# Reordering the first loads of a Strassen cross-network kernel, and holding back its first writes

## The chip, the cores and the metric

The kernel runs on one core of one Trainium2 chip. The metric is the device time of one execution, in microseconds; lower is better. Before the change it took 2280.2 us (median of 3 runs, 2279.63 to 2280.74).

## The reference, cut to what matters

```python
B, F, D, L = 16384, 100, 16, 6
Din = min(F * D, 1024)                       # 1024
# x0: (16384, 1024), ws: (6, 1024, 1024), bs: (6, 1024), all bf16
def reference(x0, ws, bs):
    x = x0
    for l in range(6):
        proj = jnp.einsum('bd,de->be', x, ws[l]) + bs[l]
        x = x0 * proj + x
    return x
```

## The kernel before

The batch is cut into 16 pairs of 512-row blocks. One *unit* is one layer of one pair: units 0 to 5 are the six layers of the first pair, units 6 to 11 those of the second, and so on, 96 in all. Each unit multiplies a 1024x1024 activation block by a 1024x1024 weight by Strassen's scheme. The weight's quadrants are called `1`, `w12`, `2` and `4`; seven products P1 to P7 use quadrants or sums of them. The sums (*combinations*) are `5 = w12 + 4`, `6 = 5 - 1`, `7 = 1 - w12`, `3 = 2 - 6`, and `2i` and `5i`, sums inside `2` and `5` for a second level of the scheme that later pairs use. The activation side has sums T1 to T4. In the first pair VectorE (DVE) makes the weight combinations, and the GpSimd queue writes them to the DRAM tensor `Lc`, from which later pairs load them.

All operations are put in one list with a rank each; an engine issues its operations in order of rank, so a rank table is the order of each engine.

```python
    # how the first pair makes and writes combinations
    RAW = [("1", "load"), ("2", "load"), ("4", "load"), ("w12", "stage")]     # order of a layer's raw loads
    def combo(name, w, a, b, o_, deps, ...):
        def fn():
            t = ring_make(u, w)
            tt(t[:], raw(a)[:], raw(b)[:], o_)                                 # DVE
            nc.gpsimd.dma_start(Lc[...], t[:])                                 # written at once
        add(name, fn, ...)
    # ... c5 of layer 0 is made in two halves (c5, c5b); 2i and 5i go to the buffers isum[2 * (l % 2)],
    # isum[2 * (l % 2) + 1], which every second layer uses again

    # ... the start of the program
    for w in ("1", "2"):
        nc.scalar.dma_start(wt[(0, w)][:], w_src(0, w))                        # 512 KB each, ScalarE queue
    nc.scalar.dma_start(b_rows[:], bs...)                                      # 12 KB
    load_half(nc.scalar, "w12", 0)                                             # 256 KB
    load_half(nc.scalar, "4", 0)
    load_quarter(0, 0)                                                         # x0 quarters, 512 KB each,
    load_quarter(1, 0)                                                         # DMA transposes, SyncE queue
    load_quarter(0, 1)
    load_half(nc.sync, "w12", 1)
    load_half(nc.sync, "4", 1)
    load_quarter(1, 1)
    nc.tensor.matmul(pX[3][:, 0:48], lhsT=b_rows[:], rhs=ident[0:48, 0:48], ...)
    nc.vector.tensor_copy(out=b_all[:], in_=pX[3][:, 0:48])
```

In layer 0, P1 needs quadrant `1` and x0 quarter (0,0); P2 needs `2` and quarter (1,0); P5 needs the first half of combination 5 and T1 (quarter (0,1)), then the second half; P6 needs combination 6 and T2 (quarter (1,1)). So all of x0's four quarters and all four raw quadrants, 4 MB, have to land before P6.

## Time and profile before

| | before |
|---|---|
| time, median of 3 | 2280.2 us |
| span in the profile | 2279.1 us |
| TensorE busy | 2252.4 us |
| first useful matmul | 9.20 us |
| first matmul of layer 0's P5 / P6 | 17.54 / 22.12 us |
| first matmul of layer 1's P5 | 44.48 us |

Two lines of the page, before (the busy time of each engine, and the shares of the chain of work that ended last):

```profile
PE 2252.4 (99%) x12713; PEld 1263.8 (55%) x12951; DVE 2079.8 (91%) x2326; ACT 1841.2 (81%) x3228; POOL 20.0 (1%) x42
...
PE 96%; DVE 1%; SPq 1%; issue 1%; DMA 1%; ACT 0%; DVEq 0%; ACTq 0%
```

The kernel is bound by TensorE (PE). What PE waits for in the whole execution, before (who waits, for whom, us in total, times, longest):

```profile
PE pX L558 <- DMA b_rows<-in_bs_dram: 3.3, 1, 3.3
PE pX L284 <- DVE T L197: 2.6, 2, 1.5
PE pX L531 <- DVE zeros L528: 1.2, 1, 1.2
PE pX L284 <- DVE wp L197: 0.9, 1, 0.9
PE pX L396 <- DVE ti L197: 0.2, 1, 0.2
```

L558 is the small matmul with the bias rows, L284 the matmuls of P1 to P7, L531 warm-up matmuls. Where these waits stand, in the timeline, before (start us, length us, engine, line, operation, count, and in brackets the idle time before it and what ended it; `wp` is a raw weight or a combination, `w` is w12):

```profile
9.07 0.19 PE L558 MATMUL pX<-ident,b_rows 48*128 48x48 bf16 x1 [3.28 <-DMA b_rows<-in_bs_dram]
9.20 3.63 PE L284 MATMUL pA<-x0T,wp 128*128 128x512 bf16 x16
...
17.54 1.04 PE L284 MATMUL pX<-T,wp 128*128 128x512 bf16 x3 [1.15 <-DVE T L197]
...
19.52 2.76 PE L284 MATMUL pX<-T,wp 128*128 128x512 bf16 x12 [0.94 <-DVE wp L197]
...
22.12 8.80 PE L284 MATMUL pA<-T,wp 128*128 128x512 bf16 x39
...
31.73 1.23 DVE L197 TENSOR_TENSOR wp<-w,wp 128x2048 bf16<-128x2048 bf16 x1 [2.36 <-DMA w<-in_ws_dram]
...
43.21 1.23 DVE L197 TENSOR_TENSOR T<-xst 128x2048 bf16<-128x2048 bf16 x1
...
44.48 3.61 PE L284 MATMUL pX<-T,wp 128*128 128x512 bf16 x16 [1.48 <-DVE T L197]
```

Read it so: 16 matmuls of 128x512 take 3.63 us, one each 216 ns. PE starts useful work at 9.20, stops twice around P5 of layer 0, once before P5 of layer 1, and, but for 0.2 us (the `ti` line above), never again until the tail. At 31.73 DVE makes layer 1's combination 5. This stands in DVE's order before layer 0's last outputs, so the outputs, then layer 1's T1 (43.21), then PE at 44.48 are late.

### The profile page before, as it was taken

Reading aid. Unit: us, or ns where it says so; the run is one execution under the profiler, and the core shown is the slowest. Engines: PE = TensorE matmul, PEld = TensorE weight load, DVE = VectorE, ACT = ScalarE, POOL = GpSimd, SP = SyncE. Lnnn points to the kernel's source line nnn. Section 1 sums busy time; section 2 is a strip of 40 time slices with the busy share of each in tenths; the row PEclk is TensorE's granted clock in tenths of the full one; section 3 lists DMA queues with packets and bytes.
Section 4 is the critical chain, followed back from the end, with each engine's and each line's share of the span. In section 5 each row is a group of like instructions: output and inputs, shape, how many; then the busy total and the mean of one; then the engine's idle time right before and its main releaser. Section 6 shows DMA issues by size and latency. Waiting matters only on the chain.

```text
span 2279.1 us, 34736 instructions
## 1 busy us (share of the span) xinstructions
PE 2252.4 (99%) x12713; PEld 1263.8 (55%) x12951; DVE 2079.8 (91%) x2326; ACT 1841.2 (81%) x3228; POOL 20.0 (1%) x42
## 2 busy tenths in 40 slices
PE   8999999999999999999999999999999999999998
PEld 3455555555555555555555555555555555555554
DVE  6999999999999999999999999999999999999997
ACT  5678888878888888888888888888888888888887
POOL 1110000000000000000000000000000000000000
PEclk9999999999999999999999999999999999999999
DMA  9869797796977969779697796978969689696872
GB/s 276 241 232 291 271 252 266 211 311 196 247 263 215 302 212 250 258 225 283 215 263 250 226 282 214 262 252 226 284 204 285 233 230 284 195 293 227 240 241 66
DMA packets 625868, 557.01 MB, mean 244 GB/s; under 512 B 397600, under 2 KB 552224, under 8 KB 625696
## 3 DMA queue, kind: packets, MB, share of 16 engines
q1 hardware_dynamic: 617808, 534.05, 79.1%
q0 software_dynamic: 5184, 18.88, 2.1%
q10 hardware_dynamic: 2704, 1.85, 0.3%
q8 instruction: 101, 1.65, 0.3%
q14 instruction: 71, 0.58, 0.1%
HBM read 436.22 MB, written 52.43 MB: 214 GB/s over the span
## 4 chain that ended last, share of the span: by engine, by line
PE 96%; DVE 1%; SPq 1%; issue 1%; DMA 1%; ACT 0%; DVEq 0%; ACTq 0%
PE pA L284 56%; PE pX L396 24%; PE pX L284 16%; DVE ev L197 1%; SPq L534 1%; DMA w<-in_ws_dram 1%; DVE xst L197 0%; ACT ev L293 0%; DVE T L197 0%; DVE isum L197 0%; SPq L547 0%; SPq L245 0%; DVE wp L197 0%; DVE x0T L494 0%; ACT pX L289 0%
## 5 line engine op out<-in xcount | busy, mean ns | idle before, releaser
L284 PEld LDWEIGHTS <-wp 128*128 128x128 bf16 x7904 | 772.3, 98 | 843.0 <-issue 2.9
L284 PE MATMUL pA<-T,wp 128*128 128x512 bf16 x4471 | 1048.6, 379 | 7.2
L293 ACT ACTIVATE ev<-pA,b_all 128x512 bf16<-128x512 f32 x1124 | 706.2, 691 | 212.1 <-PE pA L284 166.3
L396 PEld LDWEIGHTS <-wp 128*128 128x128 bf16 x4984 | 487.0, 98 | 158.3 <-issue 16.1
L197 DVE TENSOR_TENSOR ev<-ev,x0T 128x2048 bf16<-128x2048 bf16 (+2 forms) x484 | 483.2, 1000 | 7.9 <-ACT ev L293 1.3
L197 DVE TENSOR_TENSOR xst<-ev,xst 128x2048 bf16<-128x2048 bf16 x319 | 389.2, 1220 | 18.8 <-DVE ev L197 0.5
L396 PE MATMUL pX<-ti,wp 128*128 128x256 bf16 x2848 | 397.9, 272 | 0.2 <-DVE ti L197 0.2
L197 DVE TENSOR_TENSOR ev<-ev,ev 128x2048 bf16<-128x2048 bf16 (+1 forms) x283 | 343.9, 1215 | 25.5 <-ACT ev L293 7.4
L293 ACT ACTIVATE ev<-pX,b_all 128x512 bf16<-128x512 f32 x412 | 288.9, 706 | 61.4 <-PE pX L284 51.3
L284 PE MATMUL pX<-xst,wp 128*128 128x512 bf16 x1369 | 335.8, 379 | 0.3
L284 PE MATMUL pA<-xst,wp 128*128 128x512 bf16 x1205 | 302.3, 379 | 4.0
L289 ACT COPY pX<-pA 128x512 f32<-128x512 f32 x412 | 256.7, 627 | 39.9 <-PE pA L284 39.9
L289 ACT CAST ev<-pX 128x512 bf16<-128x512 f32 x384 | 225.1, 620 | 52.2 <-ACT ev L293 37.3
L197 DVE TENSOR_TENSOR ev<-iu,ip 128x1024 bf16<-128x1024 bf16 x178 | 122.6, 689 | 120.5 <-ACT iu L289 120.4
L289 ACT COPY pX<-pX 128x512 f32<-128x512 f32 x356 | 208.7, 587 | 8.3
L289 ACT CAST iu<-pX 128x512 bf16<-128x512 f32 x356 | 197.1, 639 | 1.0 <-PE pX L396 0.9
L197 DVE TENSOR_TENSOR T<-xst 128x2048 bf16<-128x2048 bf16 x160 | 194.9, 1218 | 0.3
L197 DVE TENSOR_TENSOR T<-xst,T 128x2048 bf16<-128x2048 bf16 x160 | 194.8, 1218 | 0.2
L396 PE MATMUL pX<-T,wp 128*128 128x256 bf16 x1068 | 160.2, 273 | 0.0
L289 ACT CAST ip<-pX 128x512 bf16<-128x512 f32 x178 | 104.8, 589 | 53.7 <-PE pX L396 53.7
L396 PE MATMUL pX<-xst,wp 128*128 128x256 bf16 x888 | 133.2, 273 | 0.0
L197 DVE TENSOR_TENSOR xst<-ev,x0T 128x2048 bf16<-128x2048 bf16 x64 | 78.3, 1223 | 1.5
(44 smaller groups left out, 621.2 us busy)
## 6 DMA issues: line engine op xcount, KB each, us to landing
wp<-Lc SPq DMA_DIRECT2D x538, 512.0 KB, 4.6
wp<-in_ws_dram SPq DMA_DIRECT2D x285, 512.0 KB, 5.4
out_dram<-x0T SPq DMA_DIRECT2D x30, 1024.0 KB, 8.4
Lc<-wp POOLq DMA_DIRECT2D x24, 512.0 KB, 6.2
Lc<-isum POOLq DMA_DIRECT2D x12, 512.0 KB, 5.5
w<-in_ws_dram SPq DMA_DIRECT2D x5, 512.0 KB, 9.3
wp<-in_ws_dram ACTq DMA_DIRECT2D x2, 512.0 KB, 5.3
out_dram<-x0T SPq DMA_DIRECT2D x2, 512.0 KB, 3.4
```

Source lines behind the costliest of these rows:

```text
L197: nc.vector.tensor_tensor(out=o, in0=a, in1=b, op=op)
L284: nc.tensor.matmul(bank[:], lhsT=wt[(u, w)][:, k, m * P:(m + 1) * P], rhs=rhs[:, k, :], start=(start and k == 0), stop=(k == KH - 1), skip ...
L289: add(name, lambda: nc.scalar.copy(out=dst, in_=src), rd, wr)
L293: add(name, lambda: nc.scalar.activation(out=dst, in_=src, func=IDENT, bias=b_all[:, c:c + 1], scale=1.0), rd, wr)
L396: nc.tensor.matmul(pX[bank][:, m * NQ:(m + 1) * NQ], lhsT=wv[:, k, m * P:(m + 1) * P], rhs=rhs[:, k, :], start=(start and m == 0 and k == ...
L534: nc.sync.dma_start_transpose(out=blk(x0Ts[0], dh, n), in_=x0[n * NB:(n + 1) * NB, dh * H:(dh + 1) * H])
```

## The change

The intent is to get the first products going sooner and to keep the early writes out of the way of the loads:

- Bias rows first on the ScalarE queue, then quadrants `1` and `2`. Both halves of w12 and `4` go to the SyncE queue, after three x0 quarters.
- The writes of the first pair's combinations become operations of their own, with ranks. The six of layer 0 also wait for a *gate*, a 128x1 copy on GpSimd that reads the first quarter of layer 0's result.
- Later layers' raw weights are loaded in the order `4`, `w12`, `1`, `2`.
- New rank tables for units 0 to 7, so a new order on PE, ScalarE and DVE. In layer 0, T1 now stands before combination 5, and `2i` is finished late.

```diff
-    RAW = [("1", "load"), ("2", "load"), ("4", "load"), ("w12", "stage")]
+    RAW = [("4", "load"), ("w12", "stage"), ("1", "load"), ("2", "load")]
@@ the rank table of unit 0, its DVE part (those of units 1 to 7 are replaced likewise; PE and ScalarE parts cut)
-2i5@-7.88 2i6@-7.41 2i3@-6.94 2i7@-6.47 c5@4.62 T1@5.76 c5b@7.12 c6@7.86 T2@9.00 T3@10.13 Qm@11.27 c7@12.40 c3@13.67
-T4@14.81 Qa@15.94 5i5@17.41 5i6@19.06 ...
+2i5@-9.73 T1@3.57 2i7@4.71 2i6@5.04 c5@5.67 c5b@7.37 c6@8.11 T2@9.25 c7@10.38 T3@11.52 T4@12.65 2i3@13.79 c3@14.12
+Qm@15.26 5i5@17.53 Va@19.74 Qa@20.88 ...
@@ writes
-                    nc.gpsimd.dma_start(Lc[units[u][1], CIDX[w]].rearrange("p (k e) -> p k e", k=KH), t[:])
+            def save(w, t, rd, weights=(), l=l):
+                def fn():
+                    nc.gpsimd.dma_start(Lc[l, CIDX[w]].rearrange("p (k e) -> p k e", k=KH), t()[:])
+                if first:
+                    late.append(lambda add=add: add("s" + w, fn, rd + ["gate"], (), weights))
+                else:
+                    add("s" + w, fn, rd, (), weights)
+            if first:
+                gate = const.tile([P, 1], BF16, name="gate")
+                late.append(lambda ...: add("gate", lambda: nc.gpsimd.tensor_copy(gate[:], xst[:, 0, 0, 0:1]), [XO[0, 0]], ["gate"]))
@@ the start of the program
+    nc.scalar.dma_start(b_rows[:], bs.rearrange("l (m p) -> (l m) p", p=P))
     for w in ("1", "2"):
         nc.scalar.dma_start(wt[(0, w)][:], w_src(0, w))
-    nc.scalar.dma_start(b_rows[:], bs.rearrange("l (m p) -> (l m) p", p=P))
-    load_half(nc.scalar, "w12", 0)
-    load_half(nc.scalar, "4", 0)
     load_quarter(0, 0)
     load_quarter(1, 0)
     load_quarter(0, 1)
-    load_half(nc.sync, "w12", 1)
-    load_half(nc.sync, "4", 1)
+    for h in range(2):
+        load_half("w12", h)
+        load_half("4", h)
     load_quarter(1, 1)
@@ the bias matmul writes a bank of pA in place of pX
```

## The prediction

> **What bounds the kernel now.** TensorE. The page gives PE 2252.4 us busy of a 2279.1 us span, and the chain that ended last is 96% PE. In the timeline the 512-column matmuls start every 216 ns without a break, apart from the start-up and three gaps. The view of waits, for PE, lists 8.2 us in all: 3.3 us for the bias rows' DMA (before the first useful matmul at 9.19 us), 2.6 us in two waits for a T tile from DVE (about 1.2 us at 17.54, P5 of layer 0; about 1.5 us at 44.48, P5 of layer 1), 0.9 us for the second half of combination 5 (at 19.52). Then nothing stops PE until the tail, which the change leaves alone.
>
> So only the first 45 us can be won. After the first matmul there are about 3.5 us of gaps; ahead of it little: the bias rows (issued at 1.75, landing 7.3 us later, 9.05) end the wait, but the first x0 quarter (0.74 + 8.2 = 8.9) lands only 0.15 us sooner.
>
> **What the change moves.**
> - No arithmetic goes; one 128x1 copy on POOL is added.
> - The bias rows go ahead of the weights on the ScalarE queue. Worth 0.1 to 0.6 us.
> - 512 KB (first halves of w12 and 4) leave the ScalarE queue and come after three x0 quarters on SyncE. In the DMA view, 8 to 10 us, the ScalarE queue moved 0.47 MB and the SyncE queue 0.05 MB, while the second quarter was outstanding. [...] Quarters landed at 8.9, 12.6, 16.1 and 20.7 us. A quarter alone took about 2 us (0.48 to 0.52 MB in the stretches 10 to 12 and 12 to 14). Estimate after: 8.6, 11, 13.3, about 19.5.
> - Price: both halves of combination 5 are later. Estimate: first half of w12 and 4 landed at 15.5, combined (0.69 us) by 16.2; second by 18. P1 and P2 (3.45 us each) end at 15.6; P5 starts near 16.3 instead of 17.54.
> - P6 needs T2, hence the fourth quarter: near 21 instead of 22.12. Gain: about 1 us.
> - Writes of layer 0's combinations wait for its first result (near 27 us) and no longer compete with loads from 11.4 us on.
> - In layer 0 DVE does later combinations behind the outputs, so T1 of layer 1 should come sooner: most of the 1.5 us gap at 44.48 closes. DVE is 99% busy from 20 to 100 us (windows): a new gap of some tenths elsewhere is likely.
>
> **Sum.** About 0.3 + 0.8 + 1.3 = 2.4 us: 2277.8 us, 0.1% faster.
>
> **What would show it.** First useful matmul at 8.5 to 9.0 us, waiting for x0T or wp, not b_rows; the third quarter landed before 14.5 us; P6's first matmul 0.5 to 1.7 us sooner; the PE wait for T near 44 us under 0.5 us; no POOL write before 25 us; PE gap-free after 60 us.
>
> **What would make it wrong.** Combination 5 comes so late that P5 waits over 1 us more; the fourth quarter, behind four half loads, lands no sooner; the delayed writes pile up at 28 us and hold back layer 2's weights.
>
> Faster by over 2%: 0.003; within 2%: 0.992; slower: 0.005. Range 2275.8 to 2280.0.

The sum: 0.3 + 0.8 + 1.3 = 2.4 us.

## The result, and the profile after

| | before | after |
|---|---|---|
| time, median (4 runs each, same rounds) | 2280.47 us | 2277.05 us |
| lowest to highest | 2279.63 to 2280.99 | 2276.78 to 2277.12 |
| span in the profile | 2279.1 us | 2275.2 us |
| first useful matmul | 9.20 | 6.78 |
| first matmul of layer 0's P5 / P6 | 17.54 / 22.12 | 15.59 / 20.36 |
| first matmul of layer 1's P5 | 44.48 | 41.08 |
| first weight load of unit 9 | 228.89 | 225.15 |

The ratio is 0.9985, with a 95% interval of 0.9968 to 1.0002: the same within 2%. A ratio here is the mean time of one kernel's fast runs over that of the other's of the same rounds, so it is not quite the ratio of the medians. The four runs of each kernel do not overlap, and the medians are 3.4 us apart.

Unit 9 is the fourth layer of the second pair. Its start, found in the trace by counting weight loads on PE, serves as a mark below. From there to the start of the last unit all 14 profiles took 2016.6 to 2017.7 us, so a kernel's gain or loss is complete by then to about 1 us. The mark also leaves out the tail, where PE's clock differs from run to run (granted, over the last 10 us: 0.91 in before, 0.82 in after).

Two lines of the page, after:

```profile
PE 2265.4 (100%) x12951; PEld 1264.0 (56%) x12951; DVE 2079.9 (91%) x2326; ACT 1839.4 (81%) x3228; POOL 22.1 (1%) x43
...
PE 98%; DVE 1%; SPq 0%; DMA 0%; issue 0%; ACT 0%; DVEq 0%
```

PE looks 13 us busier in a shorter run. That is no finding: the weight loads (PEld) are 12951 in both, and the matmuls are 12713 before and 12951 after, so 238 matmul records are missing from the trace of before. PE's share of the chain rose from 96 to 98%.

What PE waits for in the whole execution, after (every line of this view):

```profile
PE pX L285 <- ACT pX L290: 1.3, 1, 1.3
PE pX L526 <- DVE zeros L523: 1.2, 1, 1.2
PE pA L285 <- DVE T L198: 0.5, 1, 0.5
PE pX L285 <- DVE wp L198: 0.5, 1, 0.5
PE pA L285 <- DMA x0T<-in_x_dram: 0.4, 1, 0.4
```

The wait for the bias rows is gone, and so is the long wait for a T. A new one of 1.3 us, for ScalarE, has come in. The timeline, after (line numbers are one higher):

```profile
6.78 3.61 PE L285 MATMUL pA<-x0T,wp 128*128 128x512 bf16 x16 [0.36 <-DMA x0T<-in_x_dram]
...
8.70 0.57 ACT L290 COPY pX<-pA 128x512 f32<-128x512 f32 x1 [5.14 <-PE pA L285]
...
11.58 0.69 ACT L294 ACTIVATE ev<-pX,b_all 128x512 bf16<-128x512 f32 x1 [2.31 <-PE pX L285]
12.16 1.56 ACT L290 COPY pX<-pA 128x512 f32<-128x512 f32 x3
...
12.81 2.85 PE L285 MATMUL pX<-x0T,wp 128*128 128x512 bf16 x12 [1.26 <-ACT pX L290]
...
15.59 1.90 PE L285 MATMUL pX<-T,wp 128*128 128x512 bf16 x8
17.98 1.90 PE L285 MATMUL pX<-T,wp 128*128 128x512 bf16 x8 [0.49 <-DVE wp L198]
...
20.36 10.52 PE L285 MATMUL pA<-T,wp 128*128 128x512 bf16 x48 [0.49 <-DVE T L198]
...
26.24 1.22 DVE L198 TENSOR_TENSOR wp<-w,wp 128x2048 bf16<-128x2048 bf16 x1
...
39.09 1.22 DVE L198 TENSOR_TENSOR T<-xst 128x2048 bf16<-128x2048 bf16 x1
...
41.08 3.62 PE L285 MATMUL pX<-T,wp 128*128 128x512 bf16 x16
```

PE starts useful work 2.4 us sooner, but it is only 1.76 us ahead at P6 (22.12 - 20.36). At layer 1's P5, where the wait has gone, it is 3.40 us ahead, and 3.74 us at unit 9. P6 is where the first layer's time is decided: from 20.36 on PE runs without a stop. P6 waited for T2, which DVE began at 19.09. Two inputs came together there within 0.1 us: the fourth quarter (landed at 19.06), and DVE's own chain from the second half of `4` (landed at 17.13) through combinations 5 and 6. At 26.24 DVE makes layer 1's combination 5 without having waited for w12; before, it did so at 31.73. T1 of layer 1 follows 12.9 us after it (39.09), before 11.5 us after it (43.21): what DVE does in between did not get shorter, it began 5.5 us sooner.

The three ScalarE lines explain the new 1.3 us. In the new order ScalarE does the evacuation of the first P2 group (E2.0, at 11.58) before the copies that the other P2 groups need (12.16). E2.0 has to wait for P2, which waits for its x0 quarter. In this trace the copies did not pass it: their sources were complete by about 10.4 us (P1's 16 matmuls ran from 6.78 for 3.61 us), ScalarE stood idle for 2.31 us before E2.0, and the first of the three copies began only at 12.16.

This wait did not set P5 here. P5's first half needs the first half of combination 5, and the trace shows DVE make it from 14.84 to 15.53. (In a_bias_third, below, it did: combination 5's first half was made by 15.39, and P5 came at 17.11, straight behind P2.)

### The profile page after: what moved, and what is told of

Read it like the earlier page. It is cut to its first block, busy times and chain, and to the rows that moved or that the text cites. A ratio compares the mean times of both kernels' runs of the same rounds, so it can differ in the third digit from the quotient of the medians.

```text
span 2275.2 us, 34978 instructions
## 1 busy us (share of the span) xinstructions
PE 2265.4 (100%) x12951; PEld 1264.0 (56%) x12951; DVE 2079.9 (91%) x2326; ACT 1839.4 (81%) x3228; POOL 22.1 (1%) x43
## 4 chain that ended last, share of the span: by engine, by line
PE 98%; DVE 1%; SPq 0%; DMA 0%; issue 0%; ACT 0%; DVEq 0%
PE pA L285 57%; PE pX L389 24%; PE pX L285 16%; DVE ev L198 1%; SPq L529 0%; DMA wp<-in_ws_dram 0%; DVE xst L198 0%; DVE T L198 0%; DVE ti L198 0%; DVE wp L198 0%; SPq L538 0%; ACT ev L294 0%; DVE x0T L487 0%; DVEq L608 0%; DVEq L198 0%
## 5 line engine op out<-in xcount | busy, mean ns | idle before, releaser
L285 PE MATMUL pA<-xst,wp 128*128 128x512 bf16 x1280 | 313.5, 379 | 0.0
L198 DVE TENSOR_TENSOR xst<-ev,x0T 128x2048 bf16<-128x2048 bf16 x64 | 78.2, 1222 | 1.6
```

What stands on the lines that cost most here:

```text
L198: nc.vector.tensor_tensor(out=o, in0=a, in1=b, op=op)
L285: nc.tensor.matmul(bank[:], lhsT=wt[(u, w)][:, k, m * P:(m + 1) * P], rhs=rhs[:, k, :], start=(start and k == 0), stop=(k == KH - 1), skip ...
```

## The experiments

All are variants of one of the two kernels, and all gave correct results. One profiled run each, unless times are told; with a single run the state of the clock cannot be told from the total. The kernel before, run beside them, took 2279.07 us, 2280.26 us and (median of 9 runs) 2280.25 us in the three batches. The columns are first matmuls, in us, except the last two.

| kernel | first useful | P5 | P6 | layer 1 P5 | unit 9 | time of the run |
|---|---|---|---|---|---|---|
| before | 9.20 | 17.54 | 22.12 | 44.48 | 228.89 | 2280.82 |
| b_bias_first | 6.94 | 18.05 | 21.87 | 44.25 | 228.98 | 2281.26 |
| b_bias_halves | 7.17 | 19.81 | 25.64 | 46.36 | 231.05 | 2283.65 |
| b_gate | 8.76 | 17.38 | 21.20 | 48.10 | 235.71 | 2288.09 |
| b_tab1 | 8.94 | 19.07 | 22.52 | 43.30 | 228.36 | 2280.34 |
| b_tab1_queues | 7.27 | 16.75 | 20.79 | 46.78 | 231.45 | 2283.99 |
| after | 6.78 | 15.59 | 20.36 | 41.08 | 225.15 | 2277.03 |
| after_again | 6.84 | 16.43 | 20.53 | 41.25 | 225.32 | 2277.22 |
| a_bias_third | 8.66 | 17.11 | 20.56 | 41.28 | 225.36 | 2277.63 |
| a_tab1 | 7.41 | 17.83 | 21.29 | 42.01 | 226.09 | 2278.31 |
| a_no_gate | 7.06 | 16.33 | 20.39 | 45.18 | 229.27 | 2281.16 |
| a_halves_act | 7.10 | 19.49 | 22.95 | 43.66 | 227.74 | 2280.39 |
| a_raw1 | 7.01 | 16.66 | 20.75 | 41.47 | 225.54 | 2277.41 |
| a_t2_split | 6.95 | 18.37 | 21.82 | 42.54 | 226.62 | 2278.29 |

Two profiles of the same kernel, after and after_again, differ by 0.84 us at P5, but by 0.17 us at P6 and at unit 9. Differences at unit 9 well above that count, where the clock was full. In six runs PE's clock was halved for a while early on (granted 0.50 from 18 to 22 us in b_bias_halves): the 16 matmuls of a product, else about 3.6 us, took 5.09 (P2 of b_bias_first), 6.00 (P5 of b_bias_halves), 5.27 (P1 of b_gate, and 5.20 in P2 of its layer 1) and 5.31 us (P1 of b_tab1), and the last 12 of P2 4.44 in place of 2.85 in a_halves_act and a_t2_split. All four single edits of the kernel before are among them, so their loss or gain is that of the edit and of the clock together.

The old load order or the old rank tables as a whole do not fit the other kernel, because the 16-slot ring of weight tiles has to be filled in exactly the order that the tables free it. So tables are exchanged for unit 0 alone, and the load order for layer 1 alone.

### Is the earlier start the gain? Bias rows first, alone; and undone, alone

b_bias_first, an edit of the kernel before:

```diff
+    nc.scalar.dma_start(b_rows[:], ...)
     for w in ("1", "2"):
         nc.scalar.dma_start(wt[(0, w)][:], w_src(0, w))
-    nc.scalar.dma_start(b_rows[:], ...)
```

> The kernel before with one edit: the bias rows are issued first on the ScalarE queue. Theory (P6 of layer 0 is set by the arrival of the last of 4 MB, not by when PE starts): first useful matmul near 7 us instead of 9.19, but P5 of layer 0 still starts within 0.4 us of 17.54 and P6 within 0.4 us of 22.12, and the profiled span stays within 0.5 us of 2279.1. Rival (the gain of the change is its earlier start): everything after moves up by 2 us and the span is near 2277.

a_bias_third, the same edit undone in the kernel after:

```diff
-    nc.scalar.dma_start(b_rows[:], ...)
     for w in ("1", "2"):
         nc.scalar.dma_start(wt[(0, w)][:], w_src(0, w))
+    nc.scalar.dma_start(b_rows[:], ...)
```

> The kernel after with the bias rows issued after the two weights. Theory (start of PE is not what sets P6): first useful matmul 8.0 to 9.2 instead of 6.78, P5 up to 0.6 us later, P6 within 0.3 us of after, unit 9 within 0.3 us of 225.15. Rival: all moves by about 2 us.

The timeline of b_bias_first, PE's lines at P1, P2, P5 and P6:

```profile
6.94 3.61 PE L284 MATMUL pA<-x0T,wp 128*128 128x512 bf16 x16
13.13 5.09 PE L284 MATMUL pX<-x0T,wp 128*128 128x512 bf16 x16 [2.58 <-DMA x0T<-in_x_dram]
18.05 3.98 PE L284 MATMUL pX<-T,wp 128*128 128x512 bf16 x16
21.87 2.32 PE L284 MATMUL pA<-T,wp 128*128 128x512 bf16 x10
```

And the timeline of a_bias_third:

```profile
8.66 3.63 PE L285 MATMUL pA<-x0T,wp 128*128 128x512 bf16 x16
...
17.11 3.62 PE L285 MATMUL pX<-T,wp 128*128 128x512 bf16 x16
20.56 3.62 PE L285 MATMUL pA<-T,wp 128*128 128x512 bf16 x16
```

The totals came as the theory has it, both ways. In b_bias_first PE starts 2.3 us sooner and spends it all waiting for the second x0 quarter; unit 9 does not move (228.98 against 228.89). P5 came 0.5 us later than before, a tenth more than the 0.4 allowed, behind a P2 at half clock; at P6 that clock can have cost 0.3 us at most, as T2 was not ready before 21.54. In a_bias_third the first matmul is 1.9 us later than after, and unit 9 only 0.2 us later, which is the scatter. But P5 came 1.5 us later (0.7 than after_again), where 0.6 was allowed, and T2 was ready at 19.52, 1.0 us before P6: here PE's own work set P6, not the loads. The fourth quarter had landed at 18.20, against 19.06 in after. So a later start of PE and an earlier last quarter cancelled each other. That the swap of the bias rows is worth about nothing is shown; that PE's start never sets P6 is not.

### The two queue edits, in the old order

b_bias_halves: the kernel before with the new order of its first loads, old tables, old writes.

```diff
+    nc.scalar.dma_start(b_rows[:], ...)
     for w in ("1", "2"):
         nc.scalar.dma_start(wt[(0, w)][:], w_src(0, w))
-    nc.scalar.dma_start(b_rows[:], ...)
-    load_half(nc.scalar, "w12", 0)
-    load_half(nc.scalar, "4", 0)
     ...                                         # three x0 quarters
-    load_half(nc.sync, "w12", 1)
-    load_half(nc.sync, "4", 1)
+    for h in range(2):
+        load_half(nc.sync, "w12", h)
+        load_half(nc.sync, "4", h)
```

> The kernel before with both queue edits (bias rows first; first halves of w12 and 4 on SyncE after three x0 quarters), old order and old writes. Theory: third quarter lands before 14.5 us, P5 starts 16 to 16.8, P6 21 to 21.8 because the 2i write still competes, gap at layer 1's P5 stays 1 to 2 us, span 2278 to 2279.3. Rival (the queue edits are the whole gain): P6 near 20.4 and span under 2277.

It lost 2.2 us (unit 9 at 231.05). Neither expectation allowed for that. The timeline of b_bias_halves shows where:

```profile
17.92 0.69 DVE L197 TENSOR_TENSOR wp<-w,wp 128x1024 bf16<-128x1024 bf16 x1 [6.62 <-DMA wp<-in_ws_dram]
18.53 1.22 DVE L197 TENSOR_TENSOR T<-x0T 128x2048 bf16<-128x2048 bf16 x1
...
19.81 6.00 PE L284 MATMUL pX<-T,wp 128*128 128x512 bf16 x16 [4.81 <-DVE T L197]
```

In the old order combination 5's first half stands before T1 on DVE. The halves of w12 and `4` now land later, so DVE sat 6.62 us before combination 5 and T1 waited behind it. The view of waits says that PE waited for T; the cause is what stood in front of T. P5 came 2.3 us later than before. In P5, PE also ran 12 matmuls at half clock: 6.00 us in place of about 3.6, as much as the whole loss at unit 9. So that the edit puts combination 5 and P5 late is shown; what this alone would have cost at unit 9 is not.

### The new order of layer 0, alone; and undone, alone

b_tab1 is the kernel before with the new rank table of unit 0. a_tab1 is the kernel after with the old one.

```diff
-EARLY = [<old unit 0>, <old units 1 to 7>]      # b_tab1
+EARLY = [<new unit 0>, <old units 1 to 7>]
-EARLY = [<new unit 0>, <new units 1 to 7>]      # a_tab1
+EARLY = [<old unit 0>, <new units 1 to 7>]
```

> The kernel before with the new order of layer 0's operations alone (the 2i combination is finished later, so its write too; T1 before combinations; combinations for later weights spread). If DVE order made the gap at 44.48 us: it closes to under 0.3 us and the span is 2276.5 to 2278. If the late w12 of layer 1 (landed at 31.6 us) made it: DVE still waits about 2 us for w12 and the gap stays over 1 us, span over 2278.

> The kernel after with layer 0's old order alone. Old order puts the first half of combination 5 before T1 on DVE: P5 waits for T1 until 16.8 or later (15.6 after), P6 20.3 to 21.0 by weight load start 19.5 to 20.3; if DVE order closed the gap of layer 1 it returns (over 0.7 us), if early w12 and gated writes closed it, it stays under 0.4 us. Unit 9 at 225.5 to 227.

The timeline of b_tab1:

```profile
29.29 1.23 DVE L197 TENSOR_TENSOR wp<-w,wp 128x2048 bf16<-128x2048 bf16 x1 [2.60 <-DMA w<-in_ws_dram]
...
42.02 1.23 DVE L197 TENSOR_TENSOR T<-xst 128x2048 bf16<-128x2048 bf16 x1
43.30 3.61 PE L284 MATMUL pX<-T,wp 128*128 128x512 bf16 x16
```

Neither expectation came true as a whole: DVE still waited 2.6 us for w12 of layer 1, yet the gap at layer 1's P5 closed, with a span of 2278.6 us. It does not show that the new order closes the gap. In DVE's order the outputs still stand behind combination 5 of layer 1, and T1 comes 12.7 us after it, not sooner than before (11.5). T1 was 1.2 us earlier than before because w12 landed earlier (29.20 against 31.63), and PE was late: it had lost about 1.7 us in P1 at half clock, and the new order has the 1.3 us ScalarE wait. P6, at 22.52, came 2.8 us after T2 was ready. The run gained 0.5 us at unit 9; without the half clock it might have gained more. a_tab1, the timeline:

```profile
17.83 3.63 PE L285 MATMUL pX<-T,wp 128*128 128x512 bf16 x16 [2.50 <-DVE T L198]
...
42.01 3.62 PE L285 MATMUL pX<-T,wp 128*128 128x512 bf16 x16
```

Here T1 is behind combination 5 again: P5 waits 2.50 us, P6 is 0.93 us later, unit 9 0.94. But no gap came back at layer 1's P5: w12 landed at 22.97, DVE did not wait for it, and T1 was ready at 41.10. By the expectation, early w12 and held-back writes closed the gap, not layer 0's order. PE's delay of 0.93 us did not hide a gap of any size: PE came to this P5 at 41.08 in after, and T1 was ready at about the same time here.

### The gate, alone; and undone, alone

b_gate: in the kernel before, the six writes of layer 0 are held until the first quarter of its result.

```diff
-                    nc.gpsimd.dma_start(Lc[...], t[:])                      # in layer 0's combos, 2i and 5i
+        if first:
+            gate = const.tile([P, 1], BF16, name="gate")
+            add("gate", lambda: nc.gpsimd.tensor_copy(gate[:], xst[:, 0, 0, 0:1]), [XO[0, 0]], ["gate"])
+            for w in ("5", "6", "7", "3"):
+                add("s" + w, <write of w>, [f"w0.{w}", "gate"], (), [w])
+            for X, s in (("2i", isum[0]), ("5i", isum[1])):
+                add("s" + X, <write of s>, [f"{X}0.{i}" for i in "5637"] + ["gate"])
```

> The kernel before with one edit: the six writes of layer 0's combinations wait for the first quarter of its result, as in the kernel after. Theory A (the write of the 2i combination, 0.5 MB between 13.6 and 15.0 us, stands ahead of the halves of w12 and 4 and of the fourth x0 quarter, and later writes slow w12 of layer 1): P6 near 20.9 instead of 22.12, the gap at 44.48 us under 0.5 us, span 2276 to 2277.6. Rival B (my prediction: no PE wait hangs on the writes): P6 and the gap stay, span within 0.5 us of 2279.1.

The first half of theory A came true: P6 was 0.92 us sooner, at 21.20. The second did not; the kernel lost 6.8 us, about 1.6 of it at half clock (the second line of the timeline). What DVE waited for from 10 to 60 us, b_gate (the longest line):

```profile
DVE isum L198 <- DMA Lc<-isum: 7.2, 1, 7.2
```

And the timeline of b_gate:

```profile
41.29 0.43 DVE L198 TENSOR_TENSOR isum<-wp 128x512 bf16<-128x512 bf16 x1 [7.17 <-DMA Lc<-isum]
...
43.00 5.20 PE L285 MATMUL pX<-xst,wp 128*128 128x512 bf16 x16 [4.37 <-DVE xst L198]
```

The buffer of layer 0's `2i` is used again for layer 2's. In the old order DVE begins layer 2's `2i` in the middle of layer 1, before layer 0's last outputs. With the write held back, the buffer was not yet free, and everything behind stood still. The new tables put that reuse later. So the gate alone was priced here together with a buffer conflict that the change does not have.

a_no_gate: the kernel after, writes not held.

```diff
-                    late.append(lambda add=add: add("s" + w, fn, rd + ["gate"], (), weights))
+                    late.append(lambda add=add: add("s" + w, fn, rd, (), weights))
```

> The kernel after without the gate: writes of layer 0's combinations go out as soon as each is made (first near 18 us). My reading (no PE wait hangs on the writes in the new order, since 2i is finished late): P6 the same as after within 0.1, no gap over 0.3 us, unit 9 at 225.0 to 225.5. Rival (the gate is worth something): layer 1's w12 and raw weights land later and unit 9 starts over 0.5 us later.

My reading fell; the rival holds. The timeline of a_no_gate:

```profile
32.57 0.42 DVE L198 TENSOR_TENSOR isum<-wp 128x512 bf16<-128x512 bf16 x1 [4.75 <-DMA wp<-in_ws_dram]
...
36.46 3.61 PE L285 MATMUL pA<-xst,wp 128*128 128x512 bf16 x16 [2.10 <-DVE xst L198]
...
45.18 3.63 PE L285 MATMUL pX<-T,wp 128*128 128x512 bf16 x16 [1.42 <-DVE T L198]
```

P6 is where it was (20.39), so the first layer does not care. But four writes went out from 18.2 us on, among the loads of layer 1's raw weights: quadrant `2`, issued at 18.76, came at 32.55, while in the kernel after it was issued at 18.82, came at 26.18, and DVE used it before 28. DVE stood 4.75 us in front of layer 0's outputs, and unit 9 is 4.1 us later (229.27 against 225.15). The gate is worth more than the whole gain, in the new order. No product of this run's first 50 us ran at half clock (16 matmuls took 3.61 to 3.63 us).

### The order and the queue edits together, without gate and new load order

b_tab1_queues is b_tab1 and b_bias_halves in one; its edit is the two diffs above together.

> The kernel before with the new order of layer 0 and both queue edits, but ungated writes, the old load order of later layers and the old orders of layers 1 to 7. If these three parts together are the gain: P5 near 15.6, P6's first load of weights near 19.5, no gap at layer 1's P5, and unit 9 (second batch pair, fourth layer) starts near 225.6 us, against 228.9 before and 225.15 after. If the gate or the new load order is needed: P6 over 20.3 or a gap of over 0.5 us in layer 1, unit 9 later than 226.5.

The timeline of b_tab1_queues:

```profile
33.22 1.23 DVE L197 TENSOR_TENSOR wp<-w,wp 128x2048 bf16<-128x2048 bf16 x1 [5.47 <-DMA w<-in_ws_dram]
...
46.78 3.61 PE L284 MATMUL pX<-T,wp 128*128 128x512 bf16 x16 [1.49 <-DVE T L197]
```

P6 came at 20.79, close to after, so for the first layer the new order and the queue edits together are nearly enough. That both are needed is not shown: each alone ran at half clock for a while, and a_tab1 and b_gate, in the old order, have P6 at 21.29 and 21.20. Then DVE waited 5.47 us for layer 1's w12, until 33.22, and PE stopped three times (2.77, 0.53 and 1.49 us) in layer 1. Unit 9: 231.45, worse than before. The clock was full here (16 matmuls took 3.61 or 3.62 us). So layer 0's new order does not close the gap at layer 1's P5 when w12 is late. a_raw1, below, has the same loads up to this w12, and the gate (it has the later layers' new tables too): w12 was issued at 19.16 and landed at 26.12; here it was issued at 19.14 and landed at 33.13.

### Where the first halves are loaded, and the order of layer 1's loads

a_halves_act puts the first halves of w12 and `4` back on the ScalarE queue; a_raw1 loads layer 1's raw weights as `1`, `2`, `4`, `w12`.

```diff
+    for w in ("w12", "4"):                                                          # a_halves_act
+        nc.scalar.dma_start(wt[(0, w)][:, :, 0:HQ], w_src(0, w)[:, :, 0:HQ])
     ...                                                                             # three x0 quarters
-    for h in range(2):
-        load_half("w12", h)
-        load_half("4", h)
+    load_half("w12", 1)
+    load_half("4", 1)
```

```diff
+    NEWRAW = [("1", "load"), ("2", "load"), ("4", "load"), ("w12", "stage")]         # a_raw1
-        ring_seq += [(u + 1, w, k) for w, k in RAW ...]
+        raw = NEWRAW if u == 0 else RAW
+        ring_seq += [(u + 1, w, k) for w, k in raw ...]
```

> The kernel after with the first halves of w12 and 4 back on the ScalarE queue, behind the two weights. If moving them was worth something: second and third x0 quarters land 1 to 2 us later, P5 starts 16.5 to 18 and unit 9 is over 0.7 us later than 225.15. Theory that the sum of bytes ahead of P6 decides: P2 and T1 about 1 us later, but combination 5's first half is there sooner, P6 within 0.5 us of after and unit 9 between 224.9 and 225.7.

> The kernel after with layer 1's four raw weights loaded in the old order (1, 2, 4, w12). Combination 5 of layer 1 needs w12 and 4 and stands in DVE's order before layer 0's last outputs. With the gate, all four land before 27 to 28 us: if that is early enough the kernel keeps its time (unit 9 at 225.0 to 225.7). If the place of w12 matters, DVE waits 1 to 2 us for it near 26 us, and PE gets a gap of 0.5 to 2 us in layer 1.

a_halves_act lost 2.6 us. The second quarter came 2.4 us later (P2 at 12.93 against 10.52; 1.5 later than in after_again), but 8 matmuls of this run ran at half clock, about 8 x 0.21 = 1.7 us. So the part of the loss that is due to the queue is not settled: at least the late quarter is real, the size is not. a_raw1 kept its time (225.54, within 0.2 us of after_again). With the gate, the place of w12 among layer 1's loads is worth nothing that these runs show.

### A candidate

P6 waited for T2. a_t2_split makes layer 0's T2 in two halves:

```diff
-        ttop("T2", T[2][:], B22, T[1][:], SUB, [XI[1, 1], "T1"], ["T2"])
+        if first:
+            for h in "ab":
+                sl = slice(0, KQ) if h == "a" else slice(KQ, KH)
+                ttop("T2" + h, T[2][:, sl], B22[:, sl], T[1][:, sl], SUB, [XI[1, 1], "T1"], ["T2" + h])
+        else:
+            ttop("T2", ...)
```

> A candidate: the kernel after with layer 0's T2 made in two halves of 128x1024 (each about 0.69 us instead of one of 1.22), so that P6's first matmuls start after the first half. P6 waited for T2 until 20.36; expected near 19.9, a wait of about 0.15 us inside P6's first group, DVE 0.15 us busier: 0.2 to 0.4 us faster than after in the same rounds. If DVE has no slack then it loses what it gained: within 0.1 us.

> The kernel after itself, unchanged, to have its times on the same chip and in the same rounds as the candidate, and a second profile, which shows how far landings and stage starts move from run to run. Expected: median 2276.5 to 2277.6, unit 9 within 0.5 us of 225.15.

Times of the same five rounds: a_t2_split 2276.84 us (2276.56 to 2278.29), after_again 2277.45 (2276.82 to 2278.36), before 2280.25 (2279.41 to 2281.5, 9 runs). The ratios to before are 0.9984 (0.9970 to 0.9998) and 0.9988 (0.9975 to 1.0000). The candidate's median is 0.6 us lower, but the ranges overlap widely, so it is not shown to be faster.

Its profiled run was its slowest, and it shows something else. The busy time of each engine in stretches of a_t2_split (after the stretch and its length, busy us and count of PE, weight loads, DVE, ScalarE and GpSimd; then the granted PE clock, the DMA share and GB/s):

```profile
10.00:14.00 4.00, 1.58 (x7) 0.48 (x6) 0.31 (x1) 1.13 (x3) 0.00 (x0) 1.00 0.97 188
14.00:18.00 4.00, 3.91 (x11) 1.46 (x11) 2.27 (x4) 2.35 (x5) 0.00 (x0) 0.57 1.19 249
18.00:22.00 4.00, 4.00 (x20) 1.80 (x19) 3.62 (x5) 1.56 (x4) 0.00 (x0) 1.00 1.01 273
```

PE had two pauses close together: 1.25 us waiting for the x0 quarter, 1.26 us for ScalarE. Then the clock fell to half from 14.50 to 17.91, and 8 matmuls took 427 ns each in place of 216. P5 came at 18.37 and P6 at 21.82, behind PE's own work, no longer behind T2. The granted clocks give the length of such a stretch in three runs: 0.57 over 4 us here, 0.84 and 0.73 over two times 4 us in b_bias_first, 0.70 and 0.87 in a_halves_act each come to about 3.4 us at half clock. b_bias_first, b_gate, b_tab1, b_bias_halves, a_halves_act and a_t2_split had one in the first 50 us; the profiles of before, after and after_again had none (granted 1.00 from 0 to 50 us in before and after). Whether the ScalarE wait, which costs nothing in the profile of after, makes a slow stretch more likely is not shown: of the nine profiles that have this wait, two fell to half clock after it (a_halves_act, a_t2_split), and b_bias_first, b_bias_halves and b_gate fell without it. A version with E2.0 moved behind the copies was not run.

## Why the prediction was right

The predicted time was 2277.8 us and the measured one 2277.05, inside the range of 2275.8 to 2280.0 (a wide one: before was 2280.47). The limit (PE), the place of the gain (the first 45 us) and the first layer's part were reasoned rightly. The largest term, the gap in layer 1, was right in size but not by the reason given, and a term that is worth nothing was in the sum: to that extent the number was luck. The points, one by one:

- **What bounds it: right.** PE was the limit, only the first 45 us could be won, and PE runs without gaps after.
- **The start: wrong in size, and in worth.** "Worth 0.1 to 0.6 us" for the bias rows: the first useful matmul came 2.4 us sooner, because the first x0 quarter landed at 6.7 us and not at the estimated 8.6. With a 12 KB load ahead, the two weights were issued later on the ScalarE queue (1.16 us, before 0.74); between 2 and 4 us that queue moved 0.16 MB, where it had moved 0.52, and the SyncE queue 0.21 MB, where it had moved 0.09. But the term should not have been in the sum at all: in b_bias_first and a_bias_third the place of the bias rows was worth 0.2 us at most at unit 9.
- **The quarters: near.** Estimated 8.6, 11, 13.3 and 19.5 us; landed at about 6.7, 10.4, 12.6 and 19.1. A quarter alone took about 2 us, as estimated (0.49 MB from 8 to 10 us in after, at 247 GB/s).
- **P5 and P6: right in direction, too small.** Expected near 16.3 and 21, measured 15.59 and 20.36 (16.43 and 20.53 in after_again). The start and P6 together were put at 0.3 + 0.8 = 1.1 us and gave 1.76. The expected window for P6 (0.5 to 1.7 us sooner) was just missed, and met by after_again (1.59).
- **The gap in layer 1: right in size, not in its reason.** It closed entirely. 1.3 us was expected; from 1.76 ahead at P6 to 3.40 at layer 1's P5 is 1.64. The reason given was DVE's order in layer 0. That order is not needed (a_tab1: no gap) and not enough (b_tab1_queues and a_no_gate have it, with a gap of 1.49 and 1.42 us). Where the gap closed at full clock, layer 1's raw weights had landed before DVE came to them: w12 at 22.6 in after and 26.1 in a_raw1, against 31.6 before and 33.1 in b_tab1_queues.
- **The gate: no term of its own.** The prediction told only that the writes no longer compete. This is the largest of the parts that were taken out of the kernel after: without it the new order loses all of the gain and more (a_no_gate, 4.1 us). The sum came out right because it counted the gap as closed, which the gate is a condition for.
- **A new gap "of some tenths" elsewhere: not where it was looked for.** DVE was to cause it between 20 and 100 us (busy for 76.8 of these 80 us before, which is 96%, not 99, and for 78.2 after); PE has no new wait there. The new wait is 1.3 us, for ScalarE, in P2; it was hidden behind combination 5.
- The sum of the terms was 2.4 us; 3.4 us was measured in the medians and 3.74 us at unit 9. The last 0.34 us arose after layer 1's P5. A wait of 0.2 us for DVE's `ti` tile, present before and absent after, is part of it; the rest was not followed up.

## What to carry to other kernels

Parts of a schedule change cannot be priced one at a time: here, each alone, bias rows first gave nothing, both queue edits lost 2.2 us, the gate lost 6.8 us and layer 0's new order gave 0.5 us (each with a stretch at half clock in it), while the whole change gave 3.7 us, and lost 4.1 us when the gate alone was taken out (at full clock). Where an engine runs its operations in the order of a table, as DVE and ScalarE did here (ScalarE's copies, ready at about 10.4 us, began at 12.16, behind E2.0), ask of each late load or late write what stands *behind* the instruction that needs it, buffer reuse included. And find the point where the last of several inputs comes together (P6 here): an earlier start before that point is worth nothing as long as the inputs set it, and when they come sooner, PE's own work can set it (a_bias_third).

## What was measured beside it, and stays open

- What went first on the ScalarE queue, and when the first quarter landed. With 12 KB first on the ScalarE queue, the SyncE queue's first 512 KB transpose landed 6.0 us after issue in after (6.0 to 6.5 in the ten runs that do so), against 8.2 us before (7.5 to 8.2 in the four others) with 512 KB first; the 12 KB themselves took 1.7 us instead of 7.3 behind two weights.
- The rate where a transpose followed plain copies on the same queue. In after, while the fourth quarter's transpose followed four copies (15.8 to 16.9 us), single packets took up to 1.18 us, where the median is 0.018, and the rate fell to about 20 GB/s; before had the same near 17 us, with packets up to 1.38 us. The cause stays open.
- When the clock fell. In a_t2_split it fell after two pauses of PE of about 1.25 us, with four matmuls between them, and in a_no_gate a pause of 2.10 us at 34.4 did not make it fall. What makes it fall is not shown.
